# Two small matrix products of a linear-attention kernel written as two column halves of 64

## The chip, the cores and the metric

The kernel runs on one core of one Trainium2 chip. The metric is device time in microseconds of one execution; the time before is the median of three runs. TensorE (PE in the profile) multiplies matrices into PSUM and loads a stationary operand for every product (PEld), VectorE is DVE, ScalarE is ACT, GpSimd is POOL, and SyncE (SP) issues most of the transfers.

## The reference, cut to what matters

For each of 8 batches and 8 heads, with 576 positions of 64 elements, the keys and queries are turned into 128 positive features (`phi`), the keys' features are multiplied with the values (`kv`), and the queries' features with that product and with the keys' sum. A gated layer follows, with three weight matrices in float64.

```python
def phi(x):
    proj = np.einsum('bhsd,md->bhsm', x, omega)
    sq = np.sum(x * x, axis=-1, keepdims=True) / 2.0
    h = proj - sq
    h = h - np.max(h, axis=-1, keepdims=True)
    return np.exp(h) / np.sqrt(m)
q_p, k_p = (phi(q_s), phi(k_s))
kv = np.einsum('bhsm,bhsd->bhmd', k_p, v)
z = np.sum(k_p, axis=2)
num = np.einsum('bhsm,bhmd->bhsd', q_p, kv)
den = np.einsum('bhsm,bhm->bhs', q_p, z)[..., None] + 1e-06
...
gate = 1.0 / (1.0 + np.exp(-(x @ w_gate)))
val = x @ w_val
return (gate * val @ w_out).astype(np.float32)
```

## The kernel before

The work has three stages that follow each other. In the first, up to about 525 us, attention runs together with the first four of twelve column tiles of the gated layer (`first_pass`, product `gv`, L240), and VectorE turns float64 weights into float32 (`from_float64`, L75 to L97, tiles `e` and `c`). In the second, `second_pass` computes the other eight column tiles with seven products in place of eight (`gw`, L341). In the third, `last` multiplies with the output weights (`po`, L454) and stores.

Attention is cut into tasks: 4 pairs of batches (u), 4 pairs of heads (p), two halves of the sequence (b), where the middle tile of 128 positions belongs half to one batch and half to the other. A `keys` task projects its tiles of positions (`pp`, L535 to L537, on both heads at once), takes the maximum on VectorE (`mx`, L541), the exponential on ScalarE (`kp`, L576) and then multiplies the features of five tiles with the values, one product for each head and tile, which accumulate in one PSUM bank (`pkv`, L584). The values have 64 columns and two columns of ones, so that the keys' sum comes out of the same product: 66 columns stream past a stationary operand of 128 feature columns. ScalarE copies the result out (`kv`, L590). A `queries` task projects, subtracts the maximum on VectorE (`h`, L605), transposes on TensorE (`pt`, L616), takes the exponential (`qp`, L618) and multiplies with `kv` (`pn`, L628), again 66 columns past 128. VectorE divides by the denominator (`den`, `inv`, `x`, L634 to L640), TensorE transposes back (`px`, L646), and the result goes to memory (`xT`), from where `load` fetches it for the gated layer.

For the middle tile, `pn` was written in two products already: 64 positions with the `kv` of one batch and 64 with that of the other, into the two halves of the partitions. These are the only 64-column products of the kernel before. `pkv` and `pn` have float32 operands, and each such product of the program stands in the trace as two records of a load and two of a matmul: 320 products of `pkv` are 640 records, and 256 whole and 64 half products of `pn` are 512 and 128.

The order of the program: up to six tasks are advanced in turn (`attention`, L672), 14 steps of attention for each half step of the gated layer (`RATE`). The framework that builds the program then moves instructions on each engine by its own scheduling, except where `pin` keeps them in the order of the code; each engine works through its queue in the order that results. `keep_busy` (L484) adds products that nobody reads, up to the time when the first columns of the gated layer can begin.

Of the kernel before, what the change touches and what calls it, by code (L numbers as in the profile page):

```python
# [20 lines left out]
P = 128  # L21
# [2 lines left out]
NP = H // 2  # L24
MID = T // 2


GROUPS = {"k": (((0, 1), (2, 3), (4,)), ((5, 6), (7, 8))), "q": (((0, 1), (2, 3)), ((4,), (5, 6), (7, 8)))}
E = D + 2
# [71 lines left out]
def attn_glu_kernel(ctx: ExitStack, tc, qT, kT, qn, kn, va, om, ident, w, out):  # L101
    nc = tc.nc
# [25 lines left out]
    def any_bank(name):  # L128

        if not cycle:  # L130
            return bank("at", name)
        cycle.append(cycle.pop(0))
        return bank(cycle[-1], name)
# [350 lines left out]
    def keep_busy(a, b, n):  # L484

        for o in unread:
            for _ in range(n):
                nc.tensor.matmul(o[:, : b.shape[1]], lhsT=a, rhs=b, start=True, stop=True)  # L488
# [61 lines left out]
    def keys(pool, u, p, b):  # L550
        v = None
        kp = {}
        if b:
            kp[MID] = kmid.pop((u, p))
        for g in projected(pool, "k", u, p, b, kT):
            if g is None:
                yield
                continue
            id_, tiles, pp, hm, s = g
            nt = len(tiles)  # L560
            if v is None:
                v = pool.tile([P, MID + 1, 2, E], F32, tag="v", bufs=VS, name=f"v{u}_{p}_{b}")
                nc.sync.dma_start(out=v, in_=va[u, p, b])
            nb = pool.tile([P, nt, 2], F32, tag="nb", bufs=6, name=f"nb{id_}")
            nc.vector.scalar_tensor_tensor(  # L565
                out=nb, in0=s, scalar=-1.0, in1=hm, op0=ALU.mult, op1=ALU.subtract
            )
            if tiles[0] == MID:
                x = pool.tile([P, 2 * nt, M], F32, tag="kmid", bufs=4, name=f"kmid{id_}")
                kmid[u, p] = x  # L570
            else:
                x = pool.tile([P, 2 * nt, M], F32, tag="kp", bufs=KPS, name=f"kp{id_}")
            for i, t in enumerate(tiles):
                kp[t] = x[:, 2 * i : 2 * i + 2, :]
                for h in range(2):
                    nc.scalar.activation(  # L576
                        out=kp[t][:, h, :], in_=pp[:, 2 * i + h, :], func=AF.Exp,
                        bias=nb[:, i, h : h + 1], scale=SCALE,
                    )
            yield  # L580
        pkv = any_bank(f"pkv{u}_{p}_{b}")[:, : 2 * E].rearrange("p (h e) -> p h e", h=2)
        for h in range(2):
            for i in range(MID + 1):
                nc.tensor.matmul(  # L584
                    pkv[:, h, :], lhsT=kp[b * MID + i][:, h, :], rhs=v[:, i, h, :],
                    start=(i == 0), stop=(i == MID),
                )
        keep_busy(kp[b * MID][:, 0, :], id_sb, UNREAD)
        kv = pool.tile([P, 2, E], F32, tag="kv", bufs=15, name=f"kv{u}_{p}_{b}")
        nc.scalar.activation(out=kv, in_=pkv, func=AF.Copy)  # L590
        kvs[u, p, b] = kv
        yield

    def queries(pool, u, p, b):
        for g in projected(pool, "q", u, p, b, qT):
            if g is None:
                yield
                continue
            id_, tiles, pp, hm, s = g
            nt = len(tiles)  # L600
            n = 2 * nt
            sub = pool.tile([P, nt, 2], F32, tag="sub", bufs=6, name=f"sub{id_}")
            nc.vector.tensor_tensor(out=sub, in0=s, in1=hm, op=ALU.add)
            h_sb = pool.tile([P, n, M], F32, tag="h", bufs=HS, name=f"h{id_}")
            nc.vector.scalar_tensor_tensor(  # L605
                out=h_sb,
                in0=pp,
                scalar=SCALE,
                in1=sub.rearrange("p t h -> p (t h)").unsqueeze(2).broadcast_to([P, n, M]),
                op0=ALU.mult,  # L610
                op1=ALU.subtract,
            )
            yield
            pt = any_bank(f"pt{id_}")[:, : n * P].rearrange("p (i s) -> p i s", s=P)
            for i in range(n):
                nc.tensor.transpose(out=pt[:, i, :], in_=h_sb[:, i, :], identity=id_sb)  # L616
            qp = pool.tile([P, n, P], F32, tag="qp", bufs=HS, name=f"qp{id_}")
            nc.scalar.activation(out=qp, in_=pt, func=AF.Exp)  # L618
            yield
            pn = any_bank(f"pn{id_}")[:, : n * E].rearrange("p (i e) -> p i e", e=E)  # L620
            for i, t in enumerate(tiles):
                if t == MID:
                    mine = ((0, slice(0, P // 2)), (1, slice(P // 2, P)))
                else:
                    mine = ((b, slice(0, P)),)
                for h in range(2):
                    for bb, r in mine:
                        nc.tensor.matmul(  # L628
                            pn[r, 2 * i + h, :], lhsT=qp[:, 2 * i + h, r], rhs=kvs[u, p, bb][:, h, :],
                            start=True, stop=True,  # L630
                        )
            keep_busy(qp[:, 0, :], id_sb, UNREAD)
            den = pool.tile([P, n, 1], F32, tag="den", bufs=6, name=f"den{id_}")
            nc.vector.tensor_scalar(  # L634
                out=den, in0=pn[:, :, D : D + 1], scalar1=EPS, scalar2=None, op0=ALU.add
            )
            inv = pool.tile([P, n, 1], F32, tag="inv", bufs=6, name=f"inv{id_}")
            nc.vector.reciprocal(out=inv, in_=den)
            x = pool.tile([P, n, D], F32, tag="x", bufs=XS, name=f"x{id_}")
            nc.vector.tensor_tensor(  # L640
                out=x, in0=pn[:, :, :D], in1=inv.broadcast_to([P, n, D]), op=ALU.mult
            )
            yield
            px = any_bank(f"px{id_}")[:, : nt * P]
            for i in range(nt):
                nc.tensor.transpose(  # L646
                    out=px[:, i * P : (i + 1) * P],
                    in_=x[:, 2 * i : 2 * i + 2, :].rearrange("p h d -> p (h d)"),
                    identity=id_sb,
                )  # L650
            xs = pool.tile([P, nt * P], F32, tag="xs", bufs=2, name=f"xs{id_}")
            nc.scalar.activation(out=xs, in_=px, func=AF.Copy)
            o = u * 2 * S + tiles[0] * P
            nc.scalar.dma_start(out=xT[p, :, o : o + nt * P], in_=xs)
            assert through[p] == u * T + tiles[0]
            through[p] += nt
            yield
# [211 lines left out]
```

## Time and profile before

| | us |
|---|---|
| median of 3 runs | 1263.27 |
| lowest and highest | 1262.63, 1264.18 |
| the profiled execution | 1263.86 |
| its span in the trace | 1261.7 |

The profile is of one execution. In its rows, busy time is the union of an instruction group's records, idle time is that of the engine just before the group, with what ended it. The chain of work that ended last is followed back from the last instruction. A row of the timeline gives the start of a piece, its length, the engine, the line, the operation, what is written and read, the shapes (rows by columns of the stationary operand first) and the count. A matmul's record lasts long beyond the start of the next, so what one costs on a busy engine is read from start to start.

### The profile page before, as it was taken

How to read it: one execution, taken by the hardware profiler on the slowest of the kernel's cores; microseconds unless marked ns; L12 is line 12 of the kernel's file. 1: busy time of each engine (PE TensorE's matmuls, PEld its weight loads, DVE VectorE, ACT ScalarE, POOL GpSimd, SP SyncE). 2: the span in 40 equal slices, each digit the busy share in tenths (PEclk: the TensorE clock that was granted, in tenths of full speed). 3: DMA queues.
4: the chain of work that ended last, by engine and by line, in shares of the span. 5: the costliest groups of instructions: out<-in, count | busy, mean ns of one | idle time of the engine just before them, and what ended most of it. 6: DMA issues, size and time to landing. Idle time of an engine off the chain costs nothing.

```text
span 1261.7 us, 24408 instructions
## 1 busy us (share of the span) xinstructions
PE 1180.2 (94%) x8992; PEld 1119.3 (89%) x8992; DVE 905.6 (72%) x2054; ACT 533.2 (42%) x1164; POOL 510.4 (40%) x552
## 2 busy tenths in 40 slices
PE   5878989999999999888999999999998899999998
PEld 5867878879888898667899999999998899999998
DVE  6788989898989666495566556665658687777773
ACT  4445665656545554332433222222225344343331
POOL 3553333343435231151266666666667411111110
PEclk9788999999999999898999999999999899999999
DMA  7656767766665431465423333233327676666662
GB/s 255 201 177 205 247 211 242 254 210 218 209 225 166 154 91 55 143 221 200 147 108 131 122 122 122 88 122 151 122 96 276 194 226 203 190 192 186 196 186 93
DMA packets 104951, 219.44 MB, mean 174 GB/s; under 512 B 11136, under 2 KB 42112, under 8 KB 103040
## 3 DMA queue, kind: packets, MB, share of 16 engines
q1 hardware_dynamic: 87984, 198.94, 47.7%
q10 hardware_dynamic: 16848, 18.95, 4.4%
q8 instruction: 71, 1.16, 0.4%
q14 instruction: 48, 0.39, 0.1%
HBM read 141.82 MB, written 76.02 MB: 173 GB/s over the span
## 4 chain that ended last, share of the span: by engine, by line
PE 72%; DVE 12%; DMA 5%; POOL 5%; issue 4%; ACT 2%; SPq 0%; ACTq 0%; DVEq 0%; POOLq 0%
PE gw L341 26%; PE po L454 21%; PE gv L240 9%; PE pkv L584 4%; PE pnq L628 4%; PE ptq L616 2%; DMA xT<-xsq 2%; DVE mxk L541 1%; DVE mxq L541 1%; DMA xr<-xT 1%; PE ppq L535 1%; PE pxq L646 1%; PE unread L488 1%; PE ppq L537 1%; PE ppq L536 1%
## 5 line engine op out<-in xcount | busy, mean ns | idle before, releaser
L341 PE MATMUL gw<-xl,u 128*128 128x256 f32 x3024 | 363.5, 283 | 5.6 <-DVE u L321 5.6
L341 PEld LDWEIGHTS gw<-xl,u 128*128 128x128 f32 x3024 | 362.5, 190 | 6.6 <-DVE u L321 6.4
L454 PE MATMUL po<-u,yh 128*128 128x256 f32 x1512 | 273.0, 283 | 0.0
L454 PEld LDWEIGHTS po<-u,yh 128*128 128x128 f32 x1512 | 235.4, 191 | 0.0
L454 PE MATMUL po<-u,yl 128*128 128x256 f32 x756 | 214.3, 284 | 5.4 <-POOL yl L72 4.1
L240 PE MATMUL gv<-xe,wh 128*128 128x512 f32 (+1 forms) x640 | 202.9, 390 | 3.8 <-POOL xe L72 1.9
L71 ACT ACTIVATE yh<-yr 128x896 fp32r<-128x896 f32 x108 | 100.9, 951 | 158.6 <-PE po L454 70.4
L454 PEld LDWEIGHTS po<-u,yl 128*128 128x128 f32 x756 | 144.7, 191 | 5.8 <-POOL yl L72 4.3
L240 PE MATMUL gv<-xe,wl 128*128 128x512 f32 (+1 forms) x320 | 127.2, 399 | 16.8 <-DVE ye L265 9.8
L240 PEld LDWEIGHTS gv<-xe,wh 128*128 128x128 f32 x640 | 119.0, 196 | 23.7 <-POOL xe L72 6.8
L72 DVE TENSOR_TENSOR yl<-yr,yh 128x896 fp32r<-128x896 f32 x90 | 98.3, 1101 | 44.9 <-PE po L454 35.0
L72 POOL TENSOR_TENSOR yl<-yr,yh 128x896 fp32r<-128x896 f32 x18 | 39.3, 2184 | 215.4 <-PE po L454 140.5
L321 DVE TENSOR_TENSOR u<-gw,p 128x256 f32<-128x256 f32 x144 | 60.6, 421 | 58.9 <-PE gw L341 50.8
L72 POOL TENSOR_TENSOR lok<-rawk,hik 128x256 fp32r<-128x256 f32 (+1 forms) x80 | 55.2, 697 | 110.3 <-ACT hik L71 101.1
L72 POOL TENSOR_TENSOR loq<-rawq,hiq 128x256 fp32r<-128x256 f32 (+1 forms) x80 | 55.2, 698 | 101.2 <-ACT hiq L71 99.0
L240 PEld LDWEIGHTS gv<-xe,wl 128*128 128x128 f32 x320 | 63.0, 198 | 26.9 <-DVE ye L265 11.1
L445 DVE TENSOR_TENSOR yr<-yr 128x128 f32<-128x128 f32 x144 | 62.8, 469 | 26.7 <-DMA yr<-ye 26.1
L576 ACT ACTIVATE kpk<-ppk,nbk 128x128 f32<-128x128 f32 x256 | 71.1, 383 | 19.1 <-DVE nbk L565 18.0
L584 PE MATMUL pkv<-v,kpk 128*128 128x66 f32 x512 | 74.9, 281 | 3.9 <-ACT kpk L576 3.9
L584 PEld LDWEIGHTS pkv<-v,kpk 128*128 128x128 f32 x512 | 69.9, 200 | 7.0 <-ACT kpk L576 5.6
L628 PE MATMUL pnq<-kv,qpq 128*128 128x66 f32 (+1 forms) x640 | 72.4, 268 | 2.5 <-ACT qpq L618 2.5
L72 POOL TENSOR_TENSOR xe<-xr,xe 128x512 fp32r<-128x512 f32 (+1 forms) x40 | 49.9, 1261 | 61.1 <-ACT xe L71 61.0
(120 smaller groups left out, 2217.1 us busy)
## 6 DMA issues: line engine op xcount, KB each, us to landing
yl<-yl SPq DMA_DIRECT2D x36, 896.0 KB, 3.8
yr<-yl SPq DMA_DIRECT2D x72, 448.0 KB, 3.8
xr<-xT SPq DMA_DIRECT2D x68, 256.0 KB, 3.7
c<-w SPq DMA_DIRECT2D x22, 512.0 KB, 4.6
w<-c SPq DMA_DIRECT2D x11, 1024.0 KB, 4.8
v<-va SPq DMA_DIRECT2D x32, 330.0 KB, 3.3
natk<-kn SPq DMA_DIRECT2D x36, 256.0 KB, 3.7
natq<-qn SPq DMA_DIRECT2D x36, 256.0 KB, 4.0
```

Source lines behind the costliest of these rows:

```text
L71: nc.scalar.activation(out=hi, in_=x, func=AF.Copy)
L72: (lo_engine or nc.vector).tensor_tensor(out=lo, in0=x, in1=hi.bitcast(F32), op=ALU.subtract)
L240: nc.tensor.matmul(gv, lhsT=u[:, s], rhs=v, start=(m == 0), stop=(m == 3 * KC - 1))
L321: return nc.vector.tensor_tensor(out=o, in0=a, in1=b, op=ALU.add)
L341: nc.tensor.matmul(o, lhsT=u[:, k, s], rhs=v[:, kc, :], start=(first and m == 0), stop=(m == 5), skip_group_check=not first,)
L445: nc.vector.tensor_tensor(out=raw[:, o], in0=raw[:, a], in1=raw[:, b], op=op)
L454: nc.tensor.matmul(o, lhsT=u[:, i, :], rhs=v[:, k, :], start=(j + m == 0 and n in (1, 6, 5, 4)), stop=(j == NPAIR - 1 and m == 2), skip_gr ...
L541: nc.vector.tensor_reduce(out=mx, in_=pp, axis=AX.X, op=ALU.max)
L576: nc.scalar.activation(out=kp[t][:, h, :], in_=pp[:, 2 * i + h, :], func=AF.Exp, bias=nb[:, i, h : h + 1], scale=SCALE,)
L584: nc.tensor.matmul(pkv[:, h, :], lhsT=kp[b * MID + i][:, h, :], rhs=v[:, i, h, :], start=(i == 0), stop=(i == MID),)
L616: nc.tensor.transpose(out=pt[:, i, :], in_=h_sb[:, i, :], identity=id_sb)
L628: nc.tensor.matmul(pn[r, 2 * i + h, :], lhsT=qp[:, 2 * i + h, r], rhs=kvs[u, p, bb][:, h, :], start=True, stop=True,)
```

## The change

A pair of slices, `HALVES`, names the two halves of 64 columns. Each product `pkv` is issued twice, for the first and for the second half of the 128 feature columns, into the lower and the upper 64 partitions of the same PSUM columns. Each product `pn` that was whole is issued twice in the same way, over the two halves of its 128 positions, with the same `kv`; the products of the middle tile stay as they were. Shapes of tiles, transfers and all other operations are the same in kind and number.

```diff
+HALVES = slice(0, P // 2), slice(P // 2, P)
...
         for h in range(2):
             for i in range(MID + 1):
-                nc.tensor.matmul(
-                    pkv[:, h, :], lhsT=kp[b * MID + i][:, h, :], rhs=v[:, i, h, :],
-                    start=(i == 0), stop=(i == MID),
-                )
+                for r in HALVES:
+                    nc.tensor.matmul(
+                        pkv[r, h, :], lhsT=kp[b * MID + i][:, h, r], rhs=v[:, i, h, :],
+                        start=(i == 0), stop=(i == MID),
+                    )
...
             for i, t in enumerate(tiles):
-                if t == MID:
-                    mine = ((0, slice(0, P // 2)), (1, slice(P // 2, P)))
-                else:
-                    mine = ((b, slice(0, P)),)
                 for h in range(2):
-                    for bb, r in mine:
+                    for bb, r in zip((0, 1) if t == MID else (b, b), HALVES):
                         nc.tensor.matmul(
                             pn[r, 2 * i + h, :], lhsT=qp[:, 2 * i + h, r], rhs=kvs[u, p, bb][:, h, :],
                             start=True, stop=True,
                         )
```

One line is added near the top, so that lines from L28 to L583 have a number one higher after the change. The scheduling is done anew for the changed program, and it moves other instructions too. On TensorE, taking each pair of halves as one product, some 600 of 8,310 rows stand elsewhere; on VectorE some 410 of 2,056. Two places of TensorE's queue show what there is. The first is the end of a `queries` task (u 2), a whole `keys` task (u 3, five tiles, two heads) and another `queries` task; before:

```order
L628 MATMUL pnq2_1_7_5670<-kv2_1_1_4843,qpq2_1_7_5620 128x66 x4
L584 MATMUL pkv3_0_0_5681<-v3_0_0_5362,kpk3_0_0_5366 128x66 x2
L584 MATMUL pkv3_0_0_5681<-v3_0_0_5362,kpk3_0_2_5486 128x66 x2
L584 MATMUL pkv3_0_0_5681<-v3_0_0_5362,kmidk3_0_4_5632 128x66
L584 MATMUL pkv3_0_0_5681<-v3_0_0_5362,kpk3_0_0_5366 128x66 x2
L584 MATMUL pkv3_0_0_5681<-v3_0_0_5362,kpk3_0_2_5486 128x66 x2
L584 MATMUL pkv3_0_0_5681<-v3_0_0_5362,kmidk3_0_4_5632 128x66
L628 MATMUL pnq2_0_7_5694<-kv2_0_1_4732,qpq2_0_7_5640 128x66 x4
```

The same place after, on the same engine:

```order
L626 MATMUL pnq2_1_7_6086<-kv2_1_1_5223,qpq2_1_7_6036 64x66 x8
L586 MATMUL pkv3_0_0_6101<-v3_0_0_5766,kpk3_0_0_5770 64x66 x4
L586 MATMUL pkv3_0_0_6101<-v3_0_0_5766,kpk3_0_2_5894 64x66 x4
L586 MATMUL pkv3_0_0_6101<-v3_0_0_5766,kmidk3_0_4_6048 64x66 x2
L586 MATMUL pkv3_0_0_6101<-v3_0_0_5766,kpk3_0_0_5770 64x66 x4
L586 MATMUL pkv3_0_0_6101<-v3_0_0_5766,kpk3_0_2_5894 64x66 x4
L586 MATMUL pkv3_0_0_6101<-v3_0_0_5766,kmidk3_0_4_6048 64x66 x2
L626 MATMUL pnq2_0_7_6124<-kv2_0_1_5094,qpq2_0_7_6056 64x66 x8
```

Here 18 whole products have become 36 halves that follow each other without another product between them. The second place is in the same engine's queue near the end of the third pair of batches' keys (u 2, heads' pairs 2 and 3), where products of the gated layer (`gv`) and projections (`ppq`) stand between those of `pkv`; before:

```order
L584 MATMUL pkv2_2_1_5011<-v2_2_1_4866,kmidk2_2_4_4192 128x66
L584 MATMUL pkv2_3_1_5035<-v2_3_1_4928,kmidk2_3_4_4208 128x66
L584 MATMUL pkv2_2_1_5011<-v2_2_1_4866,kpk2_2_5_4870 128x66
L240 MATMUL gv1536_1_1_5194<-xe1536_3_4892,wl1_444 128x512
L240 MATMUL gv1536_1_1_5194<-xe1536_3_4892,wh1_443 128x512
L584 MATMUL pkv2_2_1_5011<-v2_2_1_4866,kpk2_2_5_4870 128x66
L535 MATMUL ppq2_1_4_5048<-omH_71,loq2_1_4_5028 128x256
L536 MATMUL ppq2_1_4_5048<-omL_72,hiq2_1_4_5027 128x256
L537 MATMUL ppq2_1_4_5048<-omH_71,hiq2_1_4_5027 128x256
```

After:

```order
L586 MATMUL pkv2_2_1_5391<-v2_2_1_5246,kmidk2_2_4_4500 64x66 x2
L586 MATMUL pkv2_3_1_5425<-v2_3_1_5308,kmidk2_3_4_4516 64x66 x2
L241 MATMUL gv1536_1_1_5594<-xe1536_1_5266,wl1_474 128x512
L241 MATMUL gv1536_1_1_5594<-xe1536_1_5266,wh1_473 128x512 x2
L586 MATMUL pkv2_2_1_5391<-v2_2_1_5246,kpk2_2_5_5250 64x66 x2
L241 MATMUL gv1536_1_1_5594<-xe1536_2_5269,wl1_474 128x512
L241 MATMUL gv1536_1_1_5594<-xe1536_2_5269,wh1_473 128x512
L586 MATMUL pkv2_2_1_5391<-v2_2_1_5246,kpk2_2_5_5250 64x66 x2
L536 MATMUL ppq2_1_4_5448<-omH_71,loq2_1_4_5418 128x256
L537 MATMUL ppq2_1_4_5448<-omL_72,hiq2_1_4_5417 128x256
L538 MATMUL ppq2_1_4_5448<-omH_71,hiq2_1_4_5417 128x256
```

Here the halves stand in runs of two to four between products of the full 128 columns, and other parts of `gv` stand between them than before. Over the whole program the halves come to 1,216 products in 114 uninterrupted runs, where before there were 64 in 12.

| time in the trace of before at which a run's product first stands | runs after | halves in them | runs before | halves in them |
|---|---|---|---|---|
| 0 to 100 us | 8 | 136 | 0 | 0 |
| 100 to 200 | 19 | 264 | 2 | 16 |
| 200 to 400 | 59 | 480 | 7 | 32 |
| 400 to 530 | 28 | 336 | 3 | 16 |

By length, 41 of the 114 runs have fewer than 7 halves (20 of them two), 38 have eight, 11 have twelve, and 24 have more than that, together 350 halves beyond the twelfth of their run.

## Prediction

> **What bounds the kernel now.** I read the page first, for the engine that ends last, then the stretch in which the changed products stand, then single rows of that stretch for their price. From the page, the span, TensorE's line and the chain's shares by line:
>
> ```profile
> span 1261.7 us, 24408 instructions
> PE 1180.2 (94%) x8992; PEld 1119.3 (89%) x8992; DVE 905.6 (72%) x2054; ACT 533.2 (42%) x1164; POOL 510.4 (40%) x552
> PE gw L341 26%; PE po L454 21%; PE gv L240 9%; PE pkv L584 4%; PE pnq L628 4%; PE ptq L616 2%; DMA xT<-xsq 2%; DVE mxk L541 1%; DVE mxq L541 1%; DMA xr<-xT 1%; PE ppq L535 1%; PE pxq L646 1%; PE unread L488 1%; PE ppq L537 1%; PE ppq L536 1%
> ```
>
> TensorE is the engine to watch, and the two products that change hold 8% of the chain. They stand in the first 525 us alone. The same chain within that stretch, its shares by line, and the busy time of the engines by stage (stretch, length, then PE, its loads, DVE, ACT, POOL with counts, granted clock, transfers):
>
> ```profile
> by line: PE gv L240 15.6%; PE pkv L584 10.6%; PE pnq L628 9.2%; PE ptq L616 5.3%; issue 4.8%; DMA xT<-xsq 4.3%; DVE mxk L541 3.2%; DVE mxq L541 3.0%; PE ppq L535 2.0%; PE pxq L646 2.0%; PE unread L488 2.0%; PE ppq L537 1.8%; PE ppq L536 1.7
> ...
> 0.00:100.00 100.00, 71.86 (x468) 68.84 (x468) 76.50 (x174) 48.21 (x123) 47.26 (x52) 0.83 0.66 218
> 100.00:200.00 100.00, 85.43 (x704) 81.79 (x705) 86.06 (x239) 62.60 (x181) 39.28 (x48) 0.97 0.67 213
> 200.00:400.00 200.00, 192.42 (x1372) 170.13 (x1372) 181.04 (x500) 113.62 (x313) 83.47 (x96) 0.99 0.66 221
> 400.00:530.00 130.00, 124.39 (x879) 108.31 (x878) 78.95 (x232) 61.51 (x169) 32.05 (x43) 0.98 0.33 104
> 530.00:1262.00 732.00, 706.14 (x5573) 690.21 (x5572) 483.08 (x913) 247.24 (x382) 308.36 (x315) 0.98 0.48 162
> ```
>
> From 200 us on TensorE is busy 96% of the time. VectorE, at 91% from 200 to 400 us, is close behind, and from 400 on it has room (61%). Before 100 us both idle a quarter of the time. After 530 us nothing that the change touches runs, so that stage is kept as it is. Who waits for the changed products, and what TensorE itself waits for most:
>
> ```profile
> DVE denq L634 <- PE pnq L628: 31.8, 37, 3.6
> ACT kv L590 <- PE pkv L584: 31.4, 29, 2.4
> DVE mxk L541 <- PE ppk L537: 19.7, 15, 4.3
> ...
> PE ptq L616 <- DVE hq L605: 18.0, 13, 3.9
> ```
>
> VectorE waits 32 us for `pn` and ScalarE 31 us for `pkv`, so shorter products release work elsewhere; in the other direction TensorE's largest wait is 18 us for VectorE.
>
> **The change part by part: what a whole product costs.** Start to start in the timeline, the first two rows from a `keys` task and the row after them, then eight records of it ahead of a product of the gated layer:
>
> ```profile
> 404.43 1.06 PE L584 MATMUL pkv<-v,kpk 128*128 128x66 f32 x8
> 405.33 0.39 PE L584 MATMUL pkv<-v,kmidk 128*128 128x66 f32 x2
> 405.55 1.06 PE L584 MATMUL pkv<-v,kpk 128*128 128x66 f32 x8
> ...
> 295.94 1.06 PE L584 MATMUL pkv<-v,kpk 128*128 128x66 f32 x8
> 296.80 0.48 PE L240 MATMUL gv<-xe,wh 128*128 128x512 f32 x1
> ```
>
> Ten records take 405.55 - 404.43 = 1.12 us, 0.112 us each; eight ahead of another shape take 0.86, which is 0.04 less than eight times that. A run of n whole records thus costs 0.112 n - 0.04 us.
>
> **What halves cost.** The kernel before has 128 records of halves, those of the middle tile, which follow each other in the same order of lower and upper half. Its longest run, with the rows around it, and a short one:
>
> ```profile
> 132.53 0.28 PE L536 MATMUL ppk<-omL,hik 128*128 128x256 f32 x1
> 132.65 0.28 PE L537 MATMUL ppk<-omH,hik 128*128 128x256 f32 x1
> 132.85 0.92 PE L628 MATMUL pnq<-kv,qpq 128*64 128x66 f32 x24
> 133.71 0.44 PE L584 MATMUL pkv<-v,kmidk 128*128 128x66 f32 x2
> ...
> 153.11 0.45 PE L628 MATMUL pnq<-kv,qpq 128*64 128x66 f32 x8
> 153.50 0.39 PE L535 MATMUL ppk<-omH,lok 128*128 128x256 f32 x1
> 153.72 0.28 PE L536 MATMUL ppk<-omL,hik 128*128 128x256 f32 x1
> 153.84 0.28 PE L537 MATMUL ppk<-omH,hik 128*128 128x256 f32 x1
> ```
>
> 24 records take 0.86 us and 8 take 0.39, so 16 more cost 0.47: 0.0294 us each, 0.0588 for the two records of one half product. Since a whole product has two records of 0.112 and becomes two halves, four records of 0.0294 stand against two of 0.112: 0.118 against 0.224 us. The gain is 0.0532 us for each half product in a long run.
>
> Going in and out costs. The first half starts 0.20 us after the product ahead of it where the rows before step by 0.12: +0.08. Behind the run the second full product starts 0.22 us after the first where the next step is 0.12: +0.10. With the short run's own 0.39, a run of n half products costs 0.39 + 0.0588 (n - 4) + 0.18 = 0.335 + 0.0588 n. Against the n whole records that it replaces, the difference is 0.335 + 0.04 + (0.0588 - 0.112) n = **0.375 - 0.0532 n us**: a run of 7 breaks even, one of 8 gains 0.05, one of 36 gains 1.54, one of 2 loses 0.27.
>
> The Trainium skill has a rule on this, in "TensorEngine Tiling (Array Packing)", section Tiling Modes: a change of the tiling mode drains TensorE. The rows bear it out as 0.08 ahead of the run, the slow first pair inside the 0.39, and 0.10 behind it.
>
> **The sum.** The table of runs in the section on the change gives the rest. Set against the runs that exist already (the terms of before are taken off):
> - 0 to 100 us: 8 x 0.375 - 136 x 0.0532 = -4.2.
> - 100 to 200: 19 x 0.375 - 264 x 0.0532 = -6.9, less the 2 runs of 16 before (-0.1): -6.8.
> - 200 to 400: 59 x 0.375 - 480 x 0.0532 = -3.4, less the 7 runs of 32 before (+0.9): -4.3. Here the schedule cuts the keys' products into twos between parts of `gv`, and most of the gain goes into the switches.
> - 400 to 530: 28 x 0.375 - 336 x 0.0532 = -7.4, less the 3 runs of 16 before (+0.3): -7.7.
>
> TensorE's queue gets 23.0 us shorter. Not all of it reaches the end. I take half in the first stage, where TensorE idles 28 of 100 us for others' work (-2.1); two thirds in the second, where both engines are at 85% (-4.5); three quarters in the third, where TensorE is full but VectorE, at 91%, would go to 93% (-3.2); nine tenths in the fourth, where VectorE is at 61% (-6.9). That is 16.7 us. The profiled execution took 1263.86 us, 2.2 above its span and 0.6 above the median: 1263.86 - 16.7 = **1247**.
>
> Three edits with one answer: the bank and the columns of each result are the same, so ScalarE's copy and VectorE's division read what they read before; no wait is added, the last half of a product releases its reader as the whole did; TensorE's instruction count grows by 1,152 loads and as many matmuls, which I price at nothing up to the pace shown (24 in a row) and at the rival below beyond that. The new schedule also moves VectorE's rows (some 410 of 2,056) for no reason of data. No row prices that. The bound I take is one of VectorE's largest waits above, 4 us either way.
>
> **The rivals.**
> - *The pace does not hold in long runs (slower).* 24 records is the longest run of halves in the trace; the longest strings of whole records go at 0.112 us for a load and a matmul. If TensorE cannot take instructions faster than that for long, the fast 24 were fed from a queue that had filled up behind it. Beyond the twelfth half product of a run (350 of them) each would cost 2 x 0.112 = 0.224 instead of 0.059, +58 us, of which 0.8 reach the end: 1247 + 46 = 1293. It decides from 0.12 us per half on, where 350 x 0.061 x 0.8 eats the 16.7 us. For it: no longer run exists. Against it: inside the 24 nothing slows, the average of 0.0294 is that of 16 records behind the first 8. On the rate at which instructions are taken, the Trainium skill's "TensorE: Matmul & The Clock Gate" (section "Wait — 56ns, not 53.3ns?") gives a floor of about 25 ns per matmul, or about 62 ns where the sequencer's software decodes; by the first a half would keep its pace, by the second two records would cost 0.124. The 0.0294 of the trace is under the second. Chance 0.10, with 0.06 slower and 0.02 each for a mild form that leaves no change or a small gain.
> - *VectorE or the new order takes the gain.* VectorE is at 91% from 200 to 400 us, and a gain that comes in pieces of 0.05 us on TensorE turns into waits for `h` (18.0 us already). If a quarter of 23.0 arrives, 1258. For it: the two engines are nearly equal there and the schedule was moved. Against it: 12 of the 23 us lie before 100 or after 400 us, where VectorE has room. Chance 0.20 (0.16 faster, 0.03 the same, 0.01 slower).
> - *A pair of halves takes as long as a whole.* Then only switches are left: (114 - 12) x 0.375 = 38 us, with the same fractions by stage (8, 17, 52 and 25 more runs) 1.5 + 4.3 + 14.6 + 8.4 = 29: 1293. The row of 24 speaks against it, 0.86 us where 12 whole records take 1.3. The Trainium skill's "TensorEngine Tiling (Array Packing)", section Overview, would have it so: tiling helps where one dimension leaves the array partly empty, and here all 128 columns are in use. The measured pace disagrees with it. Chance 0.03.
>
> **How the numbers follow.** A measurement of this kernel tells about 0.2%, 2.5 us, from no change. The forecast has 0.65, all of it faster; with 0.02 left for a schedule that turns out worse by more than it gains, faster is 0.65 + 0.16 + 0.02 = 0.83, the same 0.05, slower 0.06 + 0.01 + 0.03 + 0.02 = 0.12. The forecast's own range is 1236 (all 23 us arrive, and 4 of the order) to 1254 (10 arrive). To leave out no more than 2 in 10, it is stretched over the second rival, to 1262.
>
> **What would show it.** The last piece of the chain in the attention stage of before is the transfer of its last result:
>
> ```profile
> 523.25 1.99 DMA xT<-xsq
> ```
>
> In the profile after, the row of 64-column `pkv` should have start to start times of 0.03 us per record inside runs, also beyond the 24th record; the first full matmuls behind a run 0.22 us apart. This transfer should start some 17 us earlier, with the stages behind it as long as now. The prediction is wrong if halves in the runs of 36 to 60 step by over 0.06 us per record, if TensorE's idle time ended by VectorE grows by over 10 us, or if a switch costs over twice 0.375.

## The result, and the profile after

The changed kernel takes 1244.22 us in the median (1242.18 to 1246.24), against 1263.47 of the kernel before on the same chip: a ratio of 0.9848 with a 95% interval of 0.9831 to 0.9865, 19.2 us less. The forecast was 1247, in a range of 1236 to 1262. The profiled execution took 1246.24 us.

The page of the changed kernel, its span, TensorE's line and the chain's shares by line:

```profile
span 1244.4 us, 26719 instructions
PE 1150.0 (92%) x10144; PEld 1064.5 (86%) x10144; DVE 909.1 (73%) x2054; ACT 531.4 (43%) x1164; POOL 516.1 (41%) x552
PE gw L342 26%; PE po L455 21%; PE gv L241 9%; PE pnq L626 3%; PE pkv L586 2%; PE ptq L618 2%; DVE mxq L542 2%; DMA xr<-xT 2%; DVE mxk L542 1%; DMA xT<-xsq 1%; DVE c L185 1%; DVE hq L607 1%; POOL xe L73 1%; PE pxq L644 1%; DVE hmq L545 1%
```

TensorE has 1,152 more matmul records and is busy 30.2 us less, of which 12.9 us came back as idle time (the span less the busy time, 81.5 before, 94.4 now): the span is 17.3 shorter. The two products fell from 8% of the chain to 5%, while the stages behind attention (`gw`, `po`) kept their shares. The engines by stage, with the same columns as before:

```profile
0.00:100.00 100.00, 63.20 (x608) 57.27 (x608) 79.66 (x179) 49.08 (x124) 48.41 (x52) 0.87 0.67 221
100.00:200.00 100.00, 86.57 (x1004) 78.48 (x1005) 92.35 (x251) 65.77 (x190) 44.94 (x53) 0.95 0.71 225
200.00:400.00 200.00, 186.11 (x1883) 150.32 (x1882) 186.29 (x517) 115.01 (x323) 86.08 (x98) 1.00 0.68 228
400.00:530.00 130.00, 125.27 (x1157) 101.89 (x1156) 80.14 (x214) 61.42 (x158) 35.31 (x41) 0.97 0.38 121
```

From 200 to 400 us TensorE and VectorE are now equally busy, 186 us each: VectorE went from 91% to 93%, as the third term of the sum had it. The waits that had carried the argument, and TensorE's largest (engine and tile that wait, what ended it, then us in total, times, longest):

```profile
PE ptq L618 <- DVE hq L607: 21.2, 17, 4.0
...
DVE denq L632 <- PE pnq L626: 17.5, 15, 2.5
DVE mxk L542 <- PE ppk L538: 13.0, 14, 4.3
...
ACT kv L592 <- PE pkv L586: 11.4, 18, 1.7
```

ScalarE's wait for `pkv` went from 31.4 to 11.4 us, VectorE's for `pn` from 31.8 to 17.5. In the other direction TensorE's wait for VectorE's `h` grew from 18.0 to 21.2, and all of its idle time that VectorE ended, summed over its waits, from 39.1 to 47.6: 8.5 of the 12.9 us that came back.

**The pace.** TensorE's rows of the changed kernel where a `queries`, a `keys` and a `queries` task follow each other without another product between them:

```profile
391.89 0.28 PE L538 MATMUL ppk<-omH,hik 128*128 128x256 f32 x1
392.10 0.69 PE L626 MATMUL pnq<-kv,qpq 128*64 128x66 f32 x16
392.62 0.64 PE L586 MATMUL pkv<-v,kpk 128*64 128x66 f32 x16
...
393.80 0.64 PE L626 MATMUL pnq<-kv,qpq 128*64 128x66 f32 x16
394.37 0.39 PE L536 MATMUL ppq<-omH,loq 128*128 128x256 f32 x1
394.59 0.28 PE L537 MATMUL ppq<-omL,hiq 128*128 128x256 f32 x1
394.71 0.28 PE L538 MATMUL ppq<-omH,hiq 128*128 128x256 f32 x1
```

The run has 72 records and lasts from 392.10 to 394.37: 2.27 us, 0.0315 each, the slow first pair included. The 16 records that end the run last 0.64 us, as long as the 16 that start at 392.62, so nothing slows down along it. The first half starts 0.21 us behind the row ahead of it, the full products behind the run step by 0.22 and then by 0.12.

**When the attention of each pair of batches ends.** Its mark is the last transposition back (`px`) of the pair. First before, then after:

```profile
191.25 0.38 PE L646 MATMUL pxq<-id_sb,xq 128*128 128x128 f32 x2
304.67 0.38 PE L646 MATMUL pxq<-id_sb,xq 128*128 128x128 f32 x2
418.86 0.41 PE L646 MATMUL pxq<-id_sb,xq 128*128 128x128 f32 x2
522.39 0.41 PE L646 MATMUL pxq<-id_sb,xq 128*128 128x128 f32 x2 [0.50 <-DVE xq L640]
```

```profile
183.63 0.41 PE L644 MATMUL pxq<-id_sb,xq 128*128 128x128 f32 x2 [0.50 <-DVE xq L638]
292.99 0.38 PE L644 MATMUL pxq<-id_sb,xq 128*128 128x128 f32 x2
403.97 0.38 PE L644 MATMUL pxq<-id_sb,xq 128*128 128x128 f32 x2
503.56 0.41 PE L644 MATMUL pxq<-id_sb,xq 128*128 128x128 f32 x2
504.42 0.35 ACTq L652 DMA_DIRECT2D xT<-xsq  x1
```

The lead is 7.6, 11.7, 14.9 and 18.8 us: every quarter of the attention adds to it, and none gives any back. The last transfer of attention starts at 504.42 against 523.25, 18.8 us earlier. Behind it 740.0 us follow, where there were 738.5 before, so 1.5 us of the lead is lost there.

### The profile page after: what moved, and what is told of

It is laid out like the page before. It is cut to its first block, busy times and chain, and to the rows that moved or that the text cites. A ratio compares the mean times of both kernels' runs of the same rounds, so it can differ in the third digit from the quotient of the medians.

```text
span 1244.4 us, 26719 instructions
## 1 busy us (share of the span) xinstructions
PE 1150.0 (92%) x10144; PEld 1064.5 (86%) x10144; DVE 909.1 (73%) x2054; ACT 531.4 (43%) x1164; POOL 516.1 (41%) x552
## 4 chain that ended last, share of the span: by engine, by line
PE 69%; DVE 15%; POOL 5%; DMA 5%; issue 3%; ACT 2%; SPq 0%; ACTq 0%; DVEq 0%; POOLq 0%
PE gw L342 26%; PE po L455 21%; PE gv L241 9%; PE pnq L626 3%; PE pkv L586 2%; PE ptq L618 2%; DVE mxq L542 2%; DMA xr<-xT 2%; DVE mxk L542 1%; DMA xT<-xsq 1%; DVE c L185 1%; DVE hq L607 1%; POOL xe L73 1%; PE pxq L644 1%; DVE hmq L545 1%
## 5 line engine op out<-in xcount | busy, mean ns | idle before, releaser
L73 DVE TENSOR_TENSOR yl<-yr,yh 128x896 fp32r<-128x896 f32 x90 | 101.7, 1144 | 34.0 <-PE po L455 21.6
L73 POOL TENSOR_TENSOR loq<-rawq,hiq 128x256 fp32r<-128x256 f32 (+1 forms) x80 | 57.7, 730 | 85.0 <-ACT hiq L72 84.7
L241 PEld LDWEIGHTS gv<-xe,wl 128*128 128x128 f32 x320 | 63.1, 198 | 25.8 <-DVE ye L266 11.4
L577 ACT ACTIVATE kpk<-ppk,nbk 128x128 f32<-128x128 f32 x256 | 70.7, 387 | 17.7 <-DVE nbk L566 16.7
L618 PE MATMUL ptq<-id_sb,hq 128*128 128x128 f32 x288 | 48.1, 288 | 28.6 <-DVE hq L607 21.2
L618 PEld LDWEIGHTS ptq<-id_sb,hq 128*128 128x128 f32 x288 | 34.1, 145 | 42.9 <-issue 25.7
L620 ACT ACTIVATE qpq<-ptq 128x512 f32<-128x512 f32 (+1 forms) x80 | 44.6, 558 | 58.3 <-PE ptq L618 56.2
```

The costliest lines, as they stand in the source:

```text
L73: (lo_engine or nc.vector).tensor_tensor(out=lo, in0=x, in1=hi.bitcast(F32), op=ALU.subtract)
L241: nc.tensor.matmul(gv, lhsT=u[:, s], rhs=v, start=(m == 0), stop=(m == 3 * KC - 1))
L577: nc.scalar.activation(out=kp[t][:, h, :], in_=pp[:, 2 * i + h, :], func=AF.Exp, bias=nb[:, i, h : h + 1], scale=SCALE,)
```

## The experiments

The theory is the prediction's sum, here called the price theory, with one reason added: a half costs little because its neighbour stands in other columns of the array. The rivals: the new order that the scheduler chose for the changed program makes the gain or part of it; or the gain comes from one of the two products alone, through the engine that waited for it. Ratios are to the kernel before on the same chip (1265.97 for the first four, 1265.25 for the next four, 1264.74 for the last four).

### One product alone

`keys_only` takes the queries' product back to its old form; `queries_only` does the same with the keys'.

```diff
-                    for bb, r in zip((0, 1) if t == MID else (b, b), HALVES):
+                    for bb, r in mine:
```

```diff
-                for r in HALVES:
-                    nc.tensor.matmul(
-                        pkv[r, h, :], lhsT=kp[b * MID + i][:, h, r], rhs=v[:, i, h, :],
...
+                nc.tensor.matmul(
+                    pkv[:, h, :], lhsT=kp[b * MID + i][:, h, :], rhs=v[:, i, h, :],
```

> Only the product of keys and values is in halves; that of the queries is whole again, but for the middle tile. The schedule made for it has 73 runs with 704 half products. Price theory (a run costs 0.375 us for going in and out, each half product saves 0.0532): 73 x 0.375 - 704 x 0.0532 = -10.1, less +1.1 for the runs of before: -11.2 us of TensorE's queue; with the 0.83 of it that reached the end in the change as a whole (19.2 of 23.0), -9.3: about 1254. Rival, the new order made the gain: then the part need not follow its price, and the time is anywhere within some 4 us of 1263, or keeps most of the 19.

> Only the product of queries with keys and values is in halves; that of keys and values is whole. 66 runs with 576 half products, 45 of them of eight. Price theory: 66 x 0.375 - 576 x 0.0532 = -5.9, less +1.1: -7.0, times 0.83: -5.8, about 1258. Rival, the new order made the gain: no relation to that price; or, if a switch costs more in runs of eight than the rows say, no gain at all (1263 or more).

Measured: 1255.26 us, ratio 0.991 (0.9887 to 0.9933), and 1256.19, 0.9912 (0.9889 to 0.9936). Each product makes about half of the gain, and their sum, 10.7 + 9.8 = 20.5 us, is the change's 19.2 within the intervals. The rival with one product falls. The queries' part brought 9.8 us where its runs were priced at 5.8; why is not shown.

### Halves that are not neighbours

`sides_apart` issues all lower halves of a task before all upper ones: the same halves with the same shapes, in another order.

```diff
-            for i in range(MID + 1):
-                for r in HALVES:
+            for r in HALVES:
+                for i in range(MID + 1):
...
-            for i, t in enumerate(tiles):
-                for h in range(2):
-                    for bb, r in zip((0, 1) if t == MID else (b, b), HALVES):
+            for side, r in enumerate(HALVES):
+                for i, t in enumerate(tiles):
+                    bb = side if t == MID else b
+                    for h in range(2):
```

> Both products in halves, but all products of the lower half ahead of all those of the upper half in each run, so that neighbours no longer take turns between the two halves of the columns. 108 runs, 1,216 half products. Theory that two loads go side by side because they aim at different halves of the array: neighbours of one side can't, each record takes about 0.055, a half product 0.110 instead of 0.059, which gains nothing over the 0.112 of a whole record, and 102 more runs than before are left at about 0.37: +38 us, with 0.83 of it 1294. Rival, that a load of 64 columns is just cheaper, whatever its neighbour: pace 0.0294 as in the change, -24.2 - 1.1 = -25.3, about 1242.

Measured: 1264.53 us, ratio 0.9985 (0.9969 to 1.0001): the gain is gone, and neither number was met. Eighty records of `pkv` in `sides_apart`:

```profile
422.52 0.74 PE L586 MATMUL pkv<-v,kpk 128*64 128x66 f32 x10
423.03 0.22 PE L586 MATMUL pkv<-v,kmidk 128*64 128x66 f32 x1
423.09 0.22 PE L586 MATMUL pkv<-v,kpk 128*64 128x66 f32 x1
423.09 0.22 PE L586 MATMUL pkv<-v,kmidk 128*64 128x66 f32 x1
423.15 0.51 PE L586 MATMUL pkv<-v,kpk 128*64 128x66 f32 x7
423.44 0.22 PE L586 MATMUL pkv<-v,kmidk 128*64 128x66 f32 x1
423.50 0.22 PE L586 MATMUL pkv<-v,kpk 128*64 128x66 f32 x1
423.50 0.22 PE L586 MATMUL pkv<-v,kmidk 128*64 128x66 f32 x1
```

Where the side changes, a record of one side (`kpk`) starts together with one of the other (`kmidk`, the last tile), both at 423.09; there are three such pairs at the change, and their unrounded starts are 1 to 5 ns apart. Records of one side step by 0.06. The run of 80 takes 3.57 us, where 80 alternating ones took 2.48 (117.35 to 119.83 in the changed kernel). So the step of 0.0588 belongs to a half of the array's columns: two records pass in it if they stand in different halves. This run shows the cause of the gain more directly than the time does. In the commonest run, eight halves (33 of the 108), nothing is left of it: from its first record to the row behind it takes 0.90 us in the median, where eight whole records take 0.81 in the kernel before and eight alternating halves 0.62 in the changed one.

### Four quarters

`quarters` goes one step further, with four slices of 32 columns.

```diff
-HALVES = slice(0, P // 2), slice(P // 2, P)
+HALVES = tuple(slice(o, o + P // 4) for o in range(0, P, P // 4))
...
-                    for bb, r in zip((0, 1) if t == MID else (b, b), HALVES):
+                    for bb, r in zip((0, 0, 1, 1) if t == MID else 4 * (b,), HALVES):
```

> Four quarters of 32 columns in place of two halves, in both products. 104 runs, 2,432 quarter products (the middle tile's too). Theory of loads side by side: four quarters load together, eight records of one whole product take about 0.06 us instead of 0.118 as halves, a quarter product 0.015 against the 0.056 that it replaces: 104 x 0.375 - 2432 x 0.041 = -61 us of TensorE's queue; with VectorE in the way from 100 to 400 us perhaps 45 arrive: about 1218. Rival, that 0.0294 us is what a record costs at least, whatever its width: 0.0588 for a quarter product against 0.056, +46 us, about 1301.

Measured: 1261.55 us, ratio 0.9967 (0.9949 to 0.9985), between the two numbers. Rows of its timeline on TensorE: four with idle time ahead of them (in brackets, with what ended it), and a run of 160 records with the row behind it:

```profile
38.85 0.28 PE L538 MATMUL ppk<-omH,hik 128*128 128x256 f32 x1 [1.32 <-issue]
...
162.85 0.31 PE L626 MATMUL pnq<-kv,qpq 128*32 128x66 f32 x4 [1.46 <-issue]
...
196.10 0.31 PE L626 MATMUL pnq<-kv,qpq 128*32 128x66 f32 x4 [2.62 <-issue]
...
232.98 0.27 PE L644 MATMUL pxq<-id_sb,xq 128*128 128x128 f32 x1 [1.89 <-issue]
...
426.36 0.67 PE L586 MATMUL pkv<-v,kpk 128*32 128x66 f32 x32
426.84 0.30 PE L586 MATMUL pkv<-v,kmidk 128*32 128x66 f32 x8
...
428.57 0.30 PE L586 MATMUL pkv<-v,kmidk 128*32 128x66 f32 x8
428.80 0.38 PE L536 MATMUL ppq<-omH,loq 128*128 128x256 f32 x1
```

The run of 160 records, 20 whole products, takes 428.80 - 426.36 = 2.44 us, as long as the 20 products take in halves (2.48). So four records pass in the time of two, and a set of neighbours costs 0.06 us whether it has two or four. Narrower gains nothing here. That the kernel is some 15 us slower than the change (0.9967 against 0.9848) is another matter. Four times TensorE stood for 1.3 to 2.6 us with nothing in the trace to wait for, 7.3 us together, which neither the kernel before nor the changed one shows. TensorE has 12,576 matmul records here against 10,144, so its instructions may have come late, but no run shows that. Its idle time that VectorE ended is 53.0 us against 47.6. What the rest is stays open; the schedule is a new one here too.

### The order turned round

The scheduler orders everything anew for each program, so the next three kernels take one other order of the keys' products, heads and tiles from the last to the first: with halves (`last_first`, made from the changed kernel), with whole products (`whole_last_first`, the same edit in the kernel before), and with halves for the keys alone (`keys_last_first`).

```diff
-        for h in range(2):
-            for i in range(MID + 1):
+        for h in (1, 0):
+            for i in reversed(range(MID + 1)):
...
-                        start=(i == 0), stop=(i == MID),
+                        start=(i == MID), stop=(i == 0),
```

> Both products in halves as in the change, but the product of keys and values goes through heads and tiles from the last to the first, so that its first half waits for the last exponential and the schedule cuts it less: 83 runs instead of 114, the same 1,216 halves, no runs of two. Price theory: 83 x 0.375 - 1216 x 0.0532 = -33.6, less +1.1: -34.7; with 0.83 of it, -29: about 1235. Rival, VectorE (92 to 94% busy from 100 to 400 us in the change) takes what is left there: then no more than the 400 to 530 part comes through, about 1241; or the later start of each product makes its readers wait, 1244 or more.

> Control: the kernel before, with whole products, and only the order of heads and tiles of the product of keys and values turned round as in last_first. No halves are added. Price theory: nothing changes but the order, 1263 within 3. Rival, the order of work is what gains: several us faster or slower.

> Only the product of keys and values in halves, in the turned order; the queries' product whole but for the middle tile. 37 runs, 704 halves. Price theory: 37 x 0.375 - 704 x 0.0532 = -23.6, less +1.1: -24.7, with 0.83 -20.5: about 1243, as fast as the change with both. Rival, the parts' gains come from elsewhere: as keys_only, 1254.

Measured: 1278.23 us, ratio 1.0109 (1.0085 to 1.0133); 1300.04, 1.0277 (1.026 to 1.0295); 1285.24, 1.016 (1.014 to 1.018). All three expectations fell, and only the control with whole products says why: this order by itself costs 34.8 us. In the kernel before the middle tile comes last among a head's products; here they begin with it. From the waits of `whole_last_first`:

```profile
PE ptq L616 <- DVE hq L605: 23.3, 21, 3.5
PE pkv L584 <- ACT kmidk L576: 13.0, 6, 5.8
```

TensorE waits 13.0 us for the middle tile's exponential, where the kernel before waits 0.6. That is a part of the 34.8. The granted clock was lower too, 0.958 in the median of its runs against 0.973 for the kernel before beside it; what share that has is not shown, and the rest was not traced. Within this order halves still gain 21.8 us, and halves for the keys alone 14.8, against this control. The change's gain does not hang on the order in which it was made, and a comparison across orders can be off by more than the whole gain.

### Halves and order taken apart

`old_order_halves` takes the kernel before as it was scheduled and replaces, in the finished program, each whole product of the two by its halves in place, waits on the first and the release on the second. `new_order_whole` is the reverse: the schedule of the changed kernel, in which neighbouring halves are joined to whole products again (72 halves stay, 64 of them the middle tile's). These edits of the finished program come down to:

```diff
+                for h in range(2):
...
+                    new.append(
+                        mybir.InstMatmult(
...
+                            is_transpose=i.is_transpose, tile_size=(P, P // 2), tile_position=(0, h * P // 2),
...
+                            ins=(v, part(x, [x.ap[0], [columns[0], P // 2]], h * P // 2 * columns[0])),
+                            outs=(part(o, [[across, P // 2], *o.ap[1:]], h * P // 2 * across),),
```

```diff
+                            is_transpose=held.is_transpose, tile_size=(P, P), tile_position=(0, 0),
...
+                            ins=(v, part(x, [x.ap[0], [x.ap[1][0], P]])),
+                            outs=(part(o, [[o.ap[0][0], P], *o.ap[1:]]),),
```

> The schedule of the kernel before, instruction for instruction, with each whole product of the two replaced in its place by its two halves once the schedule is made. So only the halves are new and nothing is moved. 121 runs, 1,216 halves. Price theory: 121 x 0.375 - 1216 x 0.0532 = -19.3, less +1.1: -20.4, with 0.83 of it -17: about 1247. Rival, the new order made most of the gain: 1258 to 1264.

> The schedule of the changed kernel with neighbouring halves put back together into whole products once the schedule is made (the middle tile's 64 halves and 8 others that do not stand side by side stay). So only the order is new. Price theory: 20 runs with 72 halves, 20 x 0.375 - 72 x 0.0532 = +3.7 less +1.1, +2.6 of TensorE's queue and an order of unknown price: 1261 to 1269. Rival, the order made most of the gain: 1244 to 1250.

Measured: 1249.55 us, ratio 0.9874 (0.9852 to 0.9897), and 1265.63, 0.9997 (0.9981 to 1.0012). The new order alone does nothing; halves alone gain 15.2 us. The change's 0.9848 and this 0.9874 have intervals that overlap, so what the order adds to the halves, some 3 us if anything, stays open. The mean granted clock was 0.971 in the profiled executions of both `old_order_halves` and the kernel before, so it has no part in the gain.

Because `old_order_halves` has every other instruction of TensorE in the same order as the kernel before, each run can be set beside itself. The run of 36 whole records, 18 products (queries, keys, queries), in the kernel before:

```profile
403.48 0.28 PE L537 MATMUL ppk<-omH,hik 128*128 128x256 f32 x1
403.59 1.00 PE L628 MATMUL pnq<-kv,qpq 128*128 128x66 f32 x8
...
407.53 0.36 PE L535 MATMUL ppq<-omH,loq 128*128 128x256 f32 x1
407.73 0.28 PE L536 MATMUL ppq<-omL,hiq 128*128 128x256 f32 x1
```

And the same run in `old_order_halves`, after the same products:

```profile
391.49 0.28 PE L573 MATMUL ppk<-omH,hik 128*128 128x256 f32 x1
391.70 0.69 PE L664 MATMUL pnq<-kv,qpq 128*64 128x66 f32 x16
...
393.95 0.38 PE L571 MATMUL ppq<-omH,loq 128*128 128x256 f32 x1
394.17 0.28 PE L572 MATMUL ppq<-omL,hiq 128*128 128x256 f32 x1
```

From the product ahead to the second one behind it is 4.25 us whole and 2.68 in halves: -1.57, where 0.375 - 0.0532 x 36 = -1.54 was forecast. The same difference for the commonest lengths and the 36, among the runs of the kernel before that are whole, by the number of whole records n (median, count of runs in parentheses):

| n | measured | 0.375 - 0.0532 n |
|---|---|---|
| 2 (22) | +0.25 | +0.27 |
| 6 (10) | +0.02 | +0.06 |
| 8 (39) | -0.08 | -0.05 |
| 12 (13) | -0.28 | -0.26 |
| 14 (4) | -0.31 | -0.37 |
| 16 (8) | -0.50 | -0.48 |
| 36 (3) | -1.57 | -1.54 |

From 2 to 36 the slope is the forecast's 0.0532, and the constant is 0.35 rather than 0.375; only the row of 14 is further off. Summed over all whole runs, the measured differences are 24.2 us of TensorE's queue, of which 15.2 arrived in the medians: 63%. By quarters of the attention it is 9.5, 6.9, 4.3 and 3.5 us local; in the profiled execution the marks of the pairs of batches move ahead by 5.5, 6.3, 2.5 and 3.4 us, 17.7 together, 73%. What does not arrive is lost mostly in the first quarter (4.0 of 6.5 us), where TensorE idles for others, while the last keeps nearly everything.

### What the ends of runs cost

Three kernels test the constant. `one_whole` leaves the third of the five tiles of `pkv` whole, in the changed kernel; `old_order_one_whole` does so in `old_order_halves`. Both cut long runs, and have about 42 more runs than their partner. `long_runs` is the changed kernel's schedule with halves joined to whole products in all runs shorter than eight halves.

```diff
-                for r in HALVES:
+                for r in (slice(0, P),) if i == 2 else HALVES:
```

```diff
-                if n != P:
+                if n != P or o.memref[:3] == "pkv" and v.offset // (2 * E) == 2:
```

```diff
+                if i is not None and i.outs[0].memref[:3] in ("pkv", "pnk", "pnq"):
+                    run.append(i.name)
+                else:
+                    short.update(run if len(run) < least else ())
```

> As the change, but of the five tiles of each product of keys and values the middle one stays whole, which cuts every run of it: 157 runs, 1,088 halves. Price theory: 157 x 0.375 - 1088 x 0.0532 = +1.0, less +1.1: no gain over the kernel before, 1261 to 1265, though nine tenths of the products are still halves. Rival, switches are mostly hidden beside other engines' work and only the number of halves counts: -58 us of pace against 65 in the change, so about 0.9 of its gain, 1246.

> As old_order_halves, but the middle of the five tiles of each product of keys and values stays whole, in the same schedule: 162 runs, 1,088 halves. Price theory: 162 x 0.375 - 1088 x 0.0532 = +2.9, less +1.1: +1.8, no gain: 1263 to 1266, 18 us above old_order_halves. Rival, that switches are partly hidden beside other waits (one_whole came out at 1254.7 where 1263 was expected): about half of that difference, 1254 to 1257.

> The schedule of the changed kernel, with halves only where at least eight stand in a row and whole products in the shorter runs (but for the middle tile): 84 runs, 1,112 halves. Price theory: 84 x 0.375 - 1112 x 0.0532 = -27.7, less +1.1: -28.8; with 0.83 -24: about 1240, 4 to 5 us under the change. Rival, the short runs stand where TensorE waits for data anyhow, and their switches cost nothing: 1244, as the change.

Measured: `one_whole` 1254.74 us, ratio 0.9926 (0.9907 to 0.9944); `old_order_one_whole` 1259.2, 0.9945 (0.9926 to 0.9963); `long_runs` 1247.2, 0.9861 (0.9836 to 0.9886). A whole tile among halves costs 10 us in either schedule (9.9 by the ratios against the change, 9.7 in the same order). Both times lie between the two numbers of their expectations. In the trace of the same order TensorE's sum goes from -24.2 to -6.8 us. Of the 17.4 lost, 6.8 are the 128 halves fewer (at 0.0532), and the other 10.6 fall on 41 more runs: 0.26 each, where the formula had 0.375. It counts too much for a cut within these products, which is the direction in which the expectation for `one_whole` missed.

Taking the short runs out brought nothing: 0.9861 against the change's 0.9848, with intervals that overlap, where a gain of some 4 us was expected and the rival had none. A run of one pair's halves (n = 2 in the table) shows +0.25 us at its place, yet all of them together do not show at the end. They may stand where TensorE would have waited anyway; that is argued from the time alone.

## Why the prediction was right

- **A whole record 0.112, a half one 0.0294.** Right, and it holds beyond the 24 records seen before: 72 records at 0.0315 each with the slow start, without slowing. The first rival, at 0.10 the gravest, fell by these rows.
- **The ends of a run, 0.375.** Right within 0.03, and yet the term that was mis-sized: 0.35 for n from 2 to 36, and it counts 102 times. By 0.35 the queue's sum would have been 23.0 + 102 x 0.025 = 25.6 us, not 23.0. It is too much for a cut by a whole product of the same kind (0.26), which the change doesn't have.
- **What arrives, 16.7 of 23.0.** It was 18.8 us at the last transfer, 17.3 in the spans of the two profiled executions and 19.2 in the medians. By stage it came close to the forecast. The first mark (191.25 before, 183.63 after) and the run of queries, keys and queries (403.59 before, 392.10 after) stand near the bounds of the stages at 200 and 400 us. From there the lead is 7.6, then 3.9 more, then 7.3 more up to the last transfer, where 6.6 (2.1 + 4.5), 3.2 and 6.9 were forecast. The shares held as well: in the unchanged order the same rows stand at 185.76, 391.70 and, for the last mark, 504.70, so that 5.5 of 9.5, 6.4 of 8.1 and 5.8 of 6.6 us of TensorE's queue arrived, 58, 79 and 88%, where the forecast took 60% of the first two stages, 75% and 90%. With 0.35 for the ends, the forecast's own shares give 18.7 us in place of 16.7. The shares were chosen by eye from the busy times, so that they fit this well is in part luck.
- **VectorE at 93%.** Right in size (186.29 of 200). The second rival, that it takes the gain, fell, but not by much: TensorE's idle time ended by VectorE grew by 8.5 us (39.1 to 47.6), 3.2 of them for `h`, where over 10 was named as the sign.
- **The new order, up to 4 us either way.** Right: 0.9997 alone. That it was so small is no rule, as the turned order's 34.8 us shows.
- **A pair as long as a whole.** It fell by the run of 72: 2.27 us, where the kernel before takes 3.94 (403.59 to 407.53) for the same products. The Trainium skill's "TensorEngine Tiling (Array Packing)", section Overview, lists as the cases in which the full array is underused that one of the three dimensions is 64 or less. Here they are 128, 128 and 66, and the gain is there all the same; the list does not say that a split of a full dimension brings nothing, as the prediction had read it. `sides_apart` shows where that would have held in part: among halves that do not alternate.
- **After the attention as long as before.** 1.5 us longer.

The forecast's mechanism was right and its size 2.8 us short in the median; between the two profiled executions, from which it was worked out, 17.6 us were gained against the 16.7 forecast.

## What to carry to other kernels

Where many small products of few columns stand behind each other on a full TensorE, and start to start follows the width of the stationary operand (here 0.112 us for 128 columns and 0.058 for 64, past the same 66 streamed columns), two products of 64 columns side by side can take half the time, provided that they alternate and stand in runs of eight or more. Here 32 columns brought nothing beyond 64. Count the runs in the order that the scheduler leaves, and price each as a gain per product less a constant for its ends; then take off what lies in stages where the engine waits for others. When an order changes with the edit, undo the edit in that same order before believing the time.

## What the runs showed of the hardware

- Records that stream 66 columns, and whose stationary operands stand in different columns of the array, start 6 to 7 ns apart in the changed kernel; in the same columns the next starts after 58 ns (64 columns, `sides_apart`) and 112 ns (128, the kernel before).
- Four records of 32 columns pass in 58 ns as two of 64 do: 2.44 us for 20 products against 2.48, 15 ns per record in the mean. Below 64 columns the step in the same columns does not shrink any more; why is not shown. The Trainium skill's "TensorE: Matmul & The Clock Gate", section "Wait — 56ns, not 53.3ns?", gives a floor of about 25 ns per matmul; across different columns of the array it did not hold.
- With 12,576 matmul records in place of 10,144 (`quarters`), TensorE stood four times for 1.3 to 2.6 us without a cause that the trace shows.
- One product in two halves between products of another shape costs 0.25 us more than a whole one at its place, and the thirty runs shorter than eight halves, twenty of them such pairs, could be joined to whole products without a measurable gain.
